# One more drain of GpSimd in the last unit of an attention and two-layer mixture-of-experts kernel

## The chip, the cores and the metric

The kernel runs on one core of one Trainium2 chip. The metric is the device time of a whole execution in microseconds. Three timed runs of the kernel before gave 915.9, 917.06 and 919.68, so its median is 917.06 us.

## The reference, cut to what matters

An attention with RMS-normed queries and keys gives 1792 rows of 768 values; two mixture-of-experts layers follow, and each sends every row through one of eight experts.

```python
x = attn_out.transpose(0, 2, 1, 3).reshape(B * S, H * D)      # 1792 x 768
# layer 1, and layer 2 with a bias per modality in its logits
e_idx = argmax(x @ w_gate, axis=1)
for e in range(8):
    mask = e_idx == e
    h = maximum(x[mask] @ w1[e], 0)          # 768 -> 1024
    out[mask] = gate[mask] * (h @ w2[e])     # 1024 -> 768
```

## The kernel before, in words

The attention takes the first 330 us. After it the rows of an expert are worked on in units of at most 304 or 128 rows. A unit (`M.unit`, with its body in `halves`) gathers its rows from DRAM with indirect DMAs of GpSimd (L340), multiplies them by `w1` in eight blocks (the first half), applies the relu, multiplies by `w2` in six blocks (the second half, tile `pl`), transposes each block back on TensorE (tile `pty`, L419), scales it on VectorE into `yr` (L420) and scatters `yr` to DRAM with one indirect DMA of GpSimd for each 128 rows (L370). The tile pool of `pty` has three buffers. The scatter of a unit is put off: it is issued in block 0 of the following unit, and that of the last unit by `M.flush()` after it.

The last six units of layer 2 are `seq`: four of up to 304 rows and two of up to 128. How many rows each expert got is known on the chip alone, so between the two halves of the last unit stands a branch (`others`, L1002) over code for experts with still more rows. With these inputs that code is not entered. Each engine jumps over it by itself, and on the way GpSimd raises the semaphores of its DMA queue by what the skipped code would have added (an instruction named INC_SWDGE_SEM in the trace). VectorE's first write of `yr` in the second half waits for semaphores that this instruction raises, since the earlier scatters must have read `yr`.

At the end of the program (L1038) SyncE waits for the last transfers, every engine runs a drain, an instruction without operands, and the engines meet in a barrier that GpSimd gathers. Then the semaphores are cleared and a second barrier follows. `side` is a table: for a unit and a step of it, functions that are called there. `pin` keeps the instructions of each engine in the order in which they were issued.

Of the kernel before, what the change touches and what calls it, by code (L numbers as in the profile page):

```python
# [805 lines left out]
def body_full(tc,q,k,v,g_q,g_k,wg,wog,w1,w2,mod,wg2,bias2,v1,v2,out,stop=False,O=None):  # L806
    nc=tc.nc
    with ExitStack() as ctx:
# [119 lines left out]
        def stepper(name):  # L928
            def f():
                if name not in S: S[name]=F[name]()  # L930
                next(S[name],None)
            return f
# [17 lines left out]
        sides={1:{KF+j:[stepper("table1")] for j in range(6)},2:{5:[stepper("pick2")]*2,**{j:[stepper("pick2")] for j in range(6,14)}},3:{2:[ns1],5:[stepper("pick3")]*2,**{j:[stepper("pick3")] for j in range(6,14)}}}  # L950
# [43 lines left out]
        def load(t,n): return nc.values_load(t[0:1,0:1],min_val=0,max_val=n)  # L994
# [10 lines left out]
                M.redo(seq[-1],None)  # L1005
            M.slot=sl; M.post=post
        def known(): S["over"]=load(over,E+G2)
        sides={0:{KF+i:[stepper("table3")] for i in range(6)},1:{2:[more]},4:{2:[known]}}
        for j,u in enumerate(seq):
            M.unit(u,nx=seq[j+1] if j<5 else None,fx=seq[j+2] if j<4 else None,side=sides.get(j),late=0,mid=others if j==5 else None)  # L1010
        M.flush()
# [30 lines left out]
```

## Time and profile before

| | us |
|---|---|
| median of three timed runs | 917.06 |
| the profiled execution, its own time | 913.84 |
| its span, first to last instruction | 912.1 |
| PE busy | 837.5 (92% of the span) |
| POOL (GpSimd) busy | 386.4 (42%) |

Times in the rows below count from the start of the span. An engine's name with a q (POOLq, SPq) stands for its sequencer: what it runs without the engine's datapath, such as waits for semaphores, branches, register moves and drains. A row of POOL ends when GpSimd has issued a transfer, not when the data has landed.

### The profile page before, as it was taken

The page shows a single profiled execution, that of the slowest core. Times are in us where ns is not written, and L with a number is a line of the kernel's source. Part 1 is how long each engine was busy: PE and PEld are TensorE (multiplying, and loading weights), DVE is VectorE, ACT ScalarE, POOL GpSimd, SP SyncE. Part 2 cuts the span into 40 slices and gives each one's busy share as a digit, 9 for nine tenths or more (in the row PEclk, how much of TensorE's full clock was granted, in tenths as well). Part 3 has the DMA queues.
Part 4 walks back from the last instruction along what each step waited for, and adds up shares of the span by engine and source line. Part 5 has one row for each costly group of instructions (what it writes and reads, how often), then busy time and mean ns, then how long its engine had stood idle before and what let it go on. Part 6 is the DMA issues. An engine that isn't in the chain of part 4 may idle for free. (4 is left out here: it accounts for less than half of the span.)

```text
span 912.1 us, 23363 instructions
## 1 busy us (share of the span) xinstructions
PE 837.5 (92%) x8881; PEld 657.4 (72%) x8898; DVE 681.6 (75%) x1416; ACT 526.2 (58%) x967; POOL 386.4 (42%) x404
## 2 busy tenths in 40 slices
PE   4699999998998899899999999989989999999974
PEld 1365766666655688777888898987767788777864
DVE  6688888888778784777797888888656686655780
ACT  4586776776766642565455666655435554544660
POOL 5686777777766522412243232343031522402110
PEclk9799999999999899899999999999999999999996
DMA  5577666666555554987659679778647797694750
GB/s 131 124 168 186 157 158 176 166 155 167 120 150 154 131 178 134 304 232 299 190 197 318 188 246 324 242 219 303 191 146 240 251 328 192 239 269 138 273 184 8
DMA packets 143939, 181.91 MB, mean 199 GB/s; under 512 B 73737, under 2 KB 111385, under 8 KB 143809
## 3 DMA queue, kind: packets, MB, share of 16 engines
q1 hardware_dynamic: 135712, 157.45, 58.4%
q0 software_dynamic: 6784, 22.32, 7.6%
q8 instruction: 73, 1.20, 0.6%
q10 hardware_dynamic: 1312, 0.47, 0.2%
q14 instruction: 58, 0.47, 0.2%
HBM read 130.12 MB, written 24.33 MB: 169 GB/s over the span
## 5 line engine op out<-in xcount | busy, mean ns | idle before, releaser
L361 PE MATMUL pl<-XT,w1h 128*128 128x304 f16 (+7 forms) x1632 | 252.3, 263 | 2.2 <-DVE hl L365 0.9
L361 PE MATMUL pl<-hh,w2h 128*128 128x304 f16 (+7 forms) x816 | 213.7, 273 | 7.3 <-DVEq L1002 3.6
L361 PE MATMUL pl<-hh,w2l 128*128 128x304 f16 (+7 forms) x816 | 213.2, 272 | 0.0
L361 PE MATMUL pl<-XT,w1l 128*128 128x304 f16 (+7 forms) x816 | 210.0, 269 | 1.3 <-DVE w1l L299 1.3
L361 PE MATMUL pl<-hl,w2h 128*128 128x0 bf16 x816 | 206.5, 258 | 2.6 <-DVE hl L365 2.6
L361 PEld LDWEIGHTS <-w2h 128*128 128x128 f16 x1632 | 151.9, 100 | 33.0 <-ACTq L972 3.9
L361 PEld LDWEIGHTS <-w1h 128*128 128x128 f16 x1632 | 149.8, 98 | 26.3 <-issue 3.4
L652 POOL TENSOR_TENSOR plo<-p 128x448 f16<-128x448 f32 x142 | 140.3, 1006 | 50.7 <-ACT p L649 47.3
L299 DVE TENSOR_TENSOR w1l<-r,w1h 128x1024 bf16<-128x1024 f32 x96 | 116.6, 1229 | 44.1 <-ACT w1h L298 43.9
L429 ACT COPY yt<-pl 128x304 f32<-128x304 f32 (+7 forms) x102 | 37.1, 364 | 152.3 <-PE pl L361 152.3
L345 POOL TENSOR_TENSOR XS<-xr,XS 128x768 bf16<-128x768 f32 (+5 forms) x27 | 47.9, 1794 | 167.8 <-ACT XS L344 156.6
L298 ACT CAST w1h<-r 128x1024 f16<-128x1024 f32 x96 | 99.6, 1054 | 0.1
L649 ACT ACTIVATE p<-pst,eb 128x896 f32<-128x896 f32 (+1 forms) x96 | 86.4, 911 | 14.2 <-PE pst L645 13.3
L361 PEld LDWEIGHTS <-w2l 128*128 128x128 bf16 x816 | 82.0, 100 | 16.5 <-issue 3.7
L364 ACT ACTIVATE hh<-pl 128x304 f16<-128x304 f32 (+7 forms) x136 | 50.4, 373 | 73.6 <-PE pl L361 70.1
L662 PE MATMUL av<-vv,p 128*128 128x65 f16 (+1 forms) x768 | 89.2, 198 | 2.0 <-ACT xrow L674 2.0
L361 PEld LDWEIGHTS <-w1l 128*128 128x128 bf16 x816 | 80.6, 99 | 14.3 <-DVE w1l L299 1.6
L662 PEld LDWEIGHTS <-p 128*128 128x128 bf16 (+1 forms) x768 | 73.2, 102 | 20.9 <-issue 14.8
L664 PE MATMUL av<-vv,plo 128*128 128x65 f16 (+1 forms) x768 | 87.4, 195 | 0.6 <-DVE plo L652 0.6
L663 PE MATMUL av<-vv,p 128*128 128x64 f16 (+1 forms) x768 | 87.9, 197 | 0.0
L626 DVE TENSOR_REDUCE m<-psm 128x2 f16<-128x896 f32 x70 | 76.0, 1086 | 8.3 <-PE psm L621 6.5
L299 DVE TENSOR_TENSOR w2l<-raw,w2h 128x768 bf16<-128x768 f32 x64 | 73.3, 1145 | 9.1 <-ACT w2h L298 8.4
(309 smaller groups left out, 1661.0 us busy)
## 6 DMA issues: line engine op xcount, KB each, us to landing
r<-in_moe_w_dram SPq DMA_DIRECT2D x96, 512.0 KB, 8.9
raw<-in_moe_w_dram SPq DMA_DIRECT2D x64, 384.0 KB, 5.5
r2a<-in_moe_w_dram SPq DMA_DIRECT2D x32, 384.0 KB, 7.5
r2b<-in_moe_w_dram SPq DMA_DIRECT2D x32, 384.0 KB, 6.6
T<-Z SPq DMA_DIRECT2D x48, 224.0 KB, 3.5
T<-Z SPq DMA_DIRECT2D x48, 112.0 KB, 3.1
yd<-zero SPq DMA_DIRECT2D x14, 384.0 KB, 3.1
rv<-in_v_dram SPq DMA_DIRECT2D x24, 192.0 KB, 3.5
```

The costliest lines, as they stand in the source:

```text
L298: if part!=1: nc.scalar.copy(h,t)
L299: if part!=0: (eng or nc.vector).tensor_tensor(out=l,in0=t,in1=h,op=ALU.subtract)
L345: if part!=0: (eng or nc.vector).tensor_tensor(out=self.XS[:m,t,1].bitcast(BF16),in0=x,in1=h,op=ALU.subtract)
L361: self.nc.tensor.matmul(o,a,b,start=i==0,stop=i==tot-1); i+=1
L364: nc.scalar.activation(h,p,AF.Relu)
L429: nc.scalar.copy(self.yt[:,db,:N],p)
L626: if t<3: nc.vector.tensor_reduce(m[:,t:t+4:3],p[:,:,:S],axis=AX.X,op=ALU.max,negate=True)
L649: self.nc.scalar.activation(self.d["P",i][:,self.u(kt)],p[:,:nn,:S],AF.Exp,bias=self.eb,scale=0.125)
L652: eng.tensor_tensor(out=self.d["L",i][:,u],in0=P[:,u],in1=self.hi(P)[:,u],op=ALU.subtract)
L662: nc.tensor.matmul(o,hh,w[:,0:65],start=kt==0,stop=False)
L663: nc.tensor.matmul(o[:,0:64],hh,w[:,65:129],start=False,stop=False)
L664: nc.tensor.matmul(o,ll,w[:,0:65],start=False,stop=kt==3)
```

## The change

One entry is added to the table `sides`: in the last unit (5), at step KF, which is the first block of its second half, `nc.gpsimd.drain` is called once.

```diff
-        sides={0:{KF+i:[stepper("table3")] for i in range(6)},1:{2:[more]},4:{2:[known]}}
+        sides={0:{KF+i:[stepper("table3")] for i in range(6)},1:{2:[more]},4:{2:[known]},5:{KF:[nc.gpsimd.drain]}}
```

The built program has one instruction more, a drain without waits or semaphores of its own, on GpSimd. All other instructions of the five engines, and their semaphores, are as before. The drain does not stand where the text of the kernel calls it. A drain reads and writes no tile, and in the built program it stands a little earlier: behind the scatter of the last unit but one and ahead of the branch over the extra units. The rows of GpSimd there, which list no drains and read the same before and now, are (`over` is the count that the branch tests, `s2ni` the first load of the code that is jumped over):

```order
L994 TENSOR_LOAD over
L370 DMA out_dram<-yr,idx_88 1792x768
L1002 COMPARE_AND_BRANCH
L994 TENSOR_LOAD s2ni
L997 COMPARE_AND_BRANCH
```

The added drain is between the second and the third of these. Where the branch lands, GpSimd has these rows, again the same in both: the instruction that raises the semaphores, the last scatter and the end of the program.

```order
L1002 UNCONDITIONAL_BRANCH
L1002 ISA
L1002 UNCONDITIONAL_BRANCH
L370 DMA out_dram<-yr,idx_85 1792x768
L1038 UNCONDITIONAL_BRANCH
```

Between the added drain and the first drain of the end GpSimd therefore issues one transfer, the last scatter.

## Rows read from the trace of the kernel before

**Rows 1.** Chain of waits from 880 us on; columns are start, length, what.

```profile
885.61 14.98 issue
900.59 1.21 POOLq L1038
```

**Rows 2.** Line L1038, the end; min/median/max in ns, first and last start.

```profile
L1038 SPq EVENT_SEMAPHORE  x13: 17/28/18507, 885.2 to 912.1; - x13
L1038 POOLq EVENT_SEMAPHORE  x4: 17/17/17, 911.3 to 912.0; - x4
L1038 POOLq DRAIN  x3: 46/109/10682, 900.6 to 911.8; - x3
L1038 SPq DRAIN  x3: 7/7/13, 904.3 to 911.5; - x3
```

**Rows 3.** Stages of the end: busy us of PE, PEld, DVE, ACT, POOL; clock, DMA share, GB/s.

```profile
902.00:904.00 2.00, 0.00 (x0) 0.00 (x0) 0.00 (x0) 0.00 (x0) 0.00 (x0) 0.57 0.21 80
904.00:911.30 7.30, 0.00 (x0) 0.00 (x0) 0.00 (x0) 0.00 (x0) 0.00 (x0) 0.50 0.00 0
911.30:912.10 0.80, 0.00 (x0) 0.00 (x0) 0.00 (x0) 0.00 (x0) 0.00 (x0) 0.50 0.00 0
```

**Rows 4.** Timeline of POOL, its last two instructions; start, length, what, idle before.

```profile
879.65 1.64 POOL L370 DMA_INDIRECT out_dram<-yr,idx  x1 [9.80 <-DVE hl L365]
900.82 0.98 POOL L370 DMA_INDIRECT out_dram<-yr,idx  x1 [19.53 <-DVE yr L420]
```

**Rows 5.** Line L1027, the start of the program; columns as in Rows 2.

```profile
L1027 POOLq INC_SWDGE_SEM  x1: 27/27/27, 0.2 to 0.2; - x1
...
L1027 POOLq DRAIN  x1: 182/182/182, 0.4 to 0.4; - x1
```

**Rows 6.** Timeline of POOL around an indirect DMA of the attention.

```profile
286.75 1.82 POOL L652 TENSOR_TENSOR plo<-p 128x448 f16<-128x448 f32 x2
288.73 1.26 POOL L155 DMA_INDIRECT o<-payc,rt_ixi  x1 [0.16 <-issue]
289.99 1.85 POOL L652 TENSOR_TENSOR plo<-p 128x448 f16<-128x448 f32 x2
```

**Rows 7.** POOL's groups of indirect DMAs; count, busy us, mean ns, idle before.

```profile
L370 POOL DMA_INDIRECT yd<-yr,idx x19 | 24.5, 1290 | 43.4 <-DMA yd<-yr,idx 21.1 <-DVE yl L432 8.1 <-DMA pay<-o 5.2
L370 POOL DMA_INDIRECT out_dram<-yr,idx x20 | 24.5, 1224 | 87.5 <-DVE yr L420 43.6 <-DMA out_dram<-yr,idx 30.8 <-DVE hl L365 12.4
L155 POOL DMA_INDIRECT o<-rt_pay,rt_ixi x19 | 22.1, 1163 | 37.1 <-DMA o<-rt_pay,rt_ixi 21.9 <-DVE hl L365 12.3 <-POOL rt_pay L144 2.9
L340 POOL DMA_INDIRECT xr<-yd,idx x20 | 21.7, 1085 | 39.2 <-DVE yr L420 19.6 <-DVE hl L365 14.8 <-issue 3.9
L340 POOL DMA_INDIRECT xr<-xd,idx x19 | 21.2, 1115 | 25.8 <-ACT lt L456 10.3 <-DVE idx L335 7.0 <-ACT hh L364 4.3
L155 POOL DMA_INDIRECT o<-payc,rt_ixi x16 | 17.6, 1097 | 28.0 <-DMA o<-payc,rt_ixi 14.7 <-DVE hl L365 8.4 <-DVE pk_mx L176 2.3
```

**Rows 8.** Line L1002, GpSimd's way over the branch; columns as in Rows 2.

```profile
L1002 POOLq EVENT_SEMAPHORE  x5: 17/43/62, 882.3 to 882.6; - x5
...
L1002 POOLq COMPARE_BRANCH  x1: 62/62/62, 879.4 to 879.4; - x1
L1002 POOLq INC_SWDGE_SEM  x1: 2450/2450/2450, 882.7 to 882.7; - x1
```

**Rows 9.** Timeline of DVE, first and last write of `yr` in the second half.

```profile
894.06 0.29 DVE L420 TENSOR_TENSOR yr<-pty,pay 128x128 f32<-128x128 f32 x1 [5.96 <-PE pty L419]
...
900.25 0.29 DVE L420 TENSOR_TENSOR yr<-pty,pay 128x128 f32<-128x128 f32 x1 [0.33 <-PE pty L419]
```

**Rows 10.** Timeline of PE, first and fourth transpose of the same half.

```profile
893.60 0.42 PE L419 MATMUL pty<-ident,yt 128*128 128x128 f32 x1
...
898.10 0.28 PE L419 MATMUL pty<-ident,yt 128*128 128x128 f32 x1
```

## The prediction

> **What bounds the kernel now.** Over the whole span TensorE does, but the change touches GpSimd in the last 33 us, so I read the end first. The chain of waits [rows 1] shows GpSimd waiting 14.98 us for the last block of `yr`, and then its drain of line L1038 as the last piece. The line itself [rows 2] gives that drain 10.682 us, from 900.59 to 911.27; the other two drains of GpSimd at the end took 0.109 and 0.046 us. I take the long one to be the first, since GpSimd's next semaphore instruction starts at 911.3. SyncE's long wait for the transfers ended at 885.2 + 18.5 = 903.7, and its first drains ran at 904.3; the second was over at about 904.4. So from 904.4 everybody waits for GpSimd. The stage table [rows 3] says what happens meanwhile: between 904.0 and 911.3 no engine is busy and the DMA engines move nothing. These 911.27 - 904.40 = 6.87 us are the time that the change can reach. After the drain 912.12 - 911.27 = 0.85 us of barriers remain.
>
> **What the long drain may be.** The last scatter ran from 900.82 to 901.80 [rows 4], and the data moved before 904 [rows 3]. The drain goes on for 911.27 - 901.80 = 9.47 us behind the scatter's row. It is not the bare instruction: a drain at the program's start, ahead of any transfer, took 0.182 us [rows 5], and the two short ones above follow a drain directly. It is not GpSimd still at work on one transfer either: in the attention an operation that needs the whole engine starts right behind an indirect DMA (288.73 + 1.26 = 289.99) and takes the usual 0.92 us [rows 6]. So it is something that a drain alone waits for or does, and that the previous drain leaves clean. Two readings fit. In the first the drain settles what all transfers since the last drain have left behind. There were 19 + 20 + 19 + 20 + 19 + 16 = 113 indirect ones [rows 7], which makes 9.47 / 113 = 0.084 us each. A cost that is paid once, at the first drain after any transfer, gives the same result. In the second reading each drain that follows a transfer, even a single one, costs some 9.5 us. No row of this trace shows a drain behind a single transfer, so the rows don't decide.
>
> The Trainium skill speaks for a third reading. PSUM — Partial Sum Buffer, section "Engine vs sequencer instructions", says that a drain waits for the engine to go fully idle, and nothing more. By that rule the added drain of an idle GpSimd does nothing for the one at the end, and the sum would be zero. The trace does not agree with the rule as it stands, since POOL's last row ended 9.47 us before the drain did [rows 2, 4].
>
> **The change part by part.** It adds one drain to GpSimd and moves nothing else. The parts are the cost where it stands, and what the drain at the end costs afterwards.
>
> Where it stands: the drain comes behind the scatter of 879.65 and ahead of the branch. In the kernel before GpSimd's sequencer reached the branch at 879.4, the scatter's row ended at 881.29 [rows 4], and the semaphore instruction ran from 882.7 to 885.2 [rows 8]. From the branch to its end are 885.2 - 879.4 = 5.8 us, most of it the way to the new code. The price of the added drain lies between 0.05 us (the shortest one in rows 2) and, behind a scatter with 112 transfers already made, the 9.47 us of the long one or more. I take 9.47, the only row of a drain behind transfers. Then it ends at 881.29 + 9.47 = 890.8, and the semaphores are raised at 890.8 + 5.8 = 896.6. Queued behind it on GpSimd is only the last scatter, which waits for `yr` until 900.59 [rows 1] and so loses nothing. VectorE is the one who waits for the semaphores: its first write of `yr` goes from 894.06 to about 896.6 and ends at 896.9 [rows 9]. Behind it stand the five other writes, of 0.29 us each, of which two are late by then and catch up. TensorE notices only when its fourth transpose at 898.10 finds none of the three `pty` buffers free [rows 10], and the first one is free at 896.9. The cost is 0 with 898.1 - 896.9 = 1.2 us to spare. Without that cover each further microsecond of the added drain would move the end by one.
>
> At the end: call f the time from the last scatter's row to the end of the last long drain, 9.47 now. Below 2.6 us (904.40 - 901.80) it no longer counts, because SyncE's wait for the landing comes last. So the gain is 9.47 - max(2.6, f). f lies between 0.05 and 9.47 by the rows, or above if another drain cost something, for which nothing speaks. Under the first reading it is 0.084 us for one transfer, or 1.9 us if the drain waits for the landing until 903.7. In both cases the gain is the full 6.87 us. I take the first reading: the cost is nowhere seen beside single transfers, though 113 of them are issued, and it is gone at the next drain.
>
> The sum is 0 + (-6.87): 913.84 - 6.87 = 906.97 us for the profiled execution, with a span near 905.2. The median of the runs shown lies 3.2 us above the profiled execution, and I forecast a median: 917.06 - 6.87 = 910.2 us.
>
> **The rivals.**
>
> No change: each drain behind a transfer costs about 9.5 us, or the drain at the end holds something of its own. For it: all rows fit, since every short drain in the trace follows either no transfer or another drain, and the added drain has a scatter behind it. Against it: 9.47 us is about ten times the 0.98 us in which the scatter was issued [rows 4], and the data had moved before 904 [rows 3]. The time is then 917.06, since the added drain itself is covered by the 1.2 us. By the PSUM page's rule above it would be the same; that is a part of this rival's chance.
>
> A part of the gain: a fixed part of 5 to 8 us in every drain behind a transfer, the rest from the backlog. f is 5 to 8, the gain 1.5 to 4.5 us, the time 912.6 to 915.6. Nothing in the rows speaks for a split, and nothing against it.
>
> Slower: the added drain holds GpSimd longer than 9.47 + 1.2 = 10.7 us behind the scatter of 879.65, for instance because the first one after 112 transfers pays more than the last one does. From that point VectorE's first write of `yr` comes too late for TensorE's fourth transpose, and TensorE stands. With twice the price, 18.94 us, the drain ends at 900.2, the first `yr` at 900.2 + 5.8 + 0.3 = 906.3, and the end moves by 906.3 - 898.1 = 8.2 us if the drain at the end is not shortened: 917.06 + 8.2 = 925.3. Shortened, the two nearly cancel. Against it: the drain of the kernel before settled as many transfers and needed 9.47.
>
> That the change does not do what it says is part of the first rival: the drain stands ahead of the branch and not in the second half, but still behind the last transfer but one, so a backlog would be settled all the same.
>
> **How the numbers follow.** The forecast has a chance of 0.50, no change 0.38, a part of the gain 0.07, slower 0.05. A change under 0.5%, here 4.6 us, can't be told from none in a measurement of this kernel. The forecast's 6.87 us lie outside that bound, and the partial gain inside it. What the scatter of the runs carries over that bound between the first two cases I leave even; 0.01 of no change may read as slower. That makes 0.50 for faster, 0.38 + 0.07 - 0.01 = 0.44 for the same and 0.05 + 0.01 = 0.06 for slower. The likeliest case has a range of its own from 908.7 to 912 us. The range for 8 in 10 takes in the forecast and most of no change: from 908.4 to 918.5; the tail of no change and the slower case are left out.
>
> **What would show it.** If right, the long drain moves to about 879.4 to 890.8, VectorE's first `yr` comes near 896.6, TensorE's transposes stay where they are, and the first drain of L1038 ends by 904, so that SyncE's drain is the last to arrive. If a drain costs 9.5 us behind any transfer, both drains will be long and the 7.3 us stretch without work stays. If the added drain is short and the last one long, the cost belongs to the end of the program or to the last transfer. The prediction is wrong if the last drain still ends more than 4.9 us behind the last scatter's row, or if TensorE waits for a `pty` buffer.

## The result and the profile after

| | before | after |
|---|---|---|
| median of six timed runs, us | 918.68 (915.9 to 919.68) | 907.74 (902.84 to 910.78) |
| ratio | | 0.9878 [0.9846, 0.991] |
| the profiled execution, us (span) | 913.84 (912.1) | 907.44 (905.7) |

The brackets behind a ratio are its 95% interval. The change made the kernel faster, as forecast. The median lies 0.66 us below the lower end of the range, and the six runs put the gain at 10.9 us where 6.9 were forecast. The trace comes first, then the question whether the rest is real.

The end of the chain of waits of the kernel after (start, length, what) has the same last piece as [rows 1]. The step to the last scatter now goes through the semaphores of L1002:

```profile
871.78 24.91 DMA out_dram<-yr,idx
896.70 0.10 POOLq L1002
897.21 3.88 issue
901.09 1.20 POOLq L1038
```

The added drain has a line of its own in the trace, L389 (columns as in [rows 2]):

```profile
L389 POOLq DRAIN  x1: 11253/11253/11253, 882.3 to 882.3; - x1
```

It ended at 893.51. The end of the program, answering to [rows 2]:

```profile
L1038 SPq EVENT_SEMAPHORE  x13: 17/28/7397, 896.8 to 905.6; - x13
L1038 POOLq EVENT_SEMAPHORE  x4: 17/17/17, 904.9 to 905.6; - x4
L1038 POOLq DRAIN  x3: 50/109/3190, 901.1 to 905.4; - x3
L1038 SPq DRAIN  x3: 7/7/13, 904.8 to 905.1; - x3
```

The long drain of 10.682 us is now one of 3.190 us, from 901.09 to 904.28. SyncE's wait for the transfers ended at 896.8 + 7.4 = 904.2, so drain and landing end together. GpSimd's last scatters, answering to [rows 4]:

```profile
882.49 1.63 POOL L370 DMA_INDIRECT out_dram<-yr,idx  x1 [9.81 <-DVE hl L365]
901.33 0.97 POOL L370 DMA_INDIRECT out_dram<-yr,idx  x1 [17.20 <-DVE yr L420]
```

The added drain ended 893.51 - 884.12 = 9.39 us behind the first of these, the drain at the end 904.28 - 902.30 = 1.98 us behind the second. The stage table (columns as in [rows 3]) has lost the stretch of 7.3 us without work. What is left of it is 1.5 us, the barriers included:

```profile
902.40:904.20 1.80, 0.00 (x0) 0.00 (x0) 0.00 (x0) 0.00 (x0) 0.00 (x0) 1.00 0.23 89
904.20:905.70 1.50, 0.00 (x0) 0.00 (x0) 0.00 (x0) 0.00 (x0) 0.00 (x0) 0.64 0.00 0
```

From the end of the last scatter's row to the end of the span were 912.12 - 901.80 = 10.32 us before, and are 905.71 - 902.30 = 3.41 us now: 6.91 us less. The scatter itself came 0.50 us later, and 6.91 - 0.50 is the difference of the two spans, 6.4 us.

GpSimd's way over the branch, answering to [rows 8]:

```profile
L1002 POOLq EVENT_SEMAPHORE  x5: 17/43/43, 896.2 to 896.5; - x5
...
L1002 POOLq COMPARE_BRANCH  x1: 62/62/62, 893.5 to 893.5; - x1
L1002 POOLq INC_SWDGE_SEM  x1: 172/172/172, 896.6 to 896.6; - x1
```

INC_SWDGE_SEM fell from 2.450 to 0.172 us, which no step of the prediction had. The writes of `yr` and the transposes, answering to [rows 9, 10]; VectorE first:

```profile
897.19 0.82 DVE L420 TENSOR_TENSOR yr<-pty,pay 128x128 f32<-128x128 f32 x3 [7.31 <-DMA out_dram<-yr,idx]
...
900.75 0.29 DVE L420 TENSOR_TENSOR yr<-pty,pay 128x128 f32<-128x128 f32 x1 [0.33 <-PE pty L419]
```

and TensorE, first, fourth and last transpose:

```profile
894.97 0.28 PE L419 MATMUL pty<-ident,yt 128*128 128x128 f32 x1
...
898.61 0.28 PE L419 MATMUL pty<-ident,yt 128*128 128x128 f32 x1
...
900.39 0.33 PE L419 MATMUL pty<-ident,yt 128*128 128x128 f32 x1 [0.29 <-ACT yt L429]
```

VectorE held three blocks back and wrote them at a stretch from 897.19. The first `pty` buffer was free at about 897.5, 1.1 us before TensorE's fourth transpose, which shows no wait. In this execution the added drain cost nothing.

Elsewhere the two executions differ by the clock. Before the end, from 850 to 890 and from there on, the kernel before:

```profile
850.00:890.00 40.00, 32.69 (x511) 29.53 (x511) 30.99 (x51) 25.79 (x50) 6.72 (x5) 0.94 0.57 198
890.00:912.00 22.00, 9.92 (x147) 9.44 (x145) 1.75 (x6) 1.59 (x6) 0.98 (x1) 0.66 0.02 8
```

and the kernel after:

```profile
850.00:890.00 40.00, 33.82 (x527) 29.76 (x527) 32.42 (x52) 27.03 (x52) 6.72 (x5) 1.00 0.64 225
890.00:905.70 15.70, 9.02 (x150) 8.62 (x150) 1.66 (x6) 1.60 (x6) 0.97 (x1) 0.86 0.05 14
```

The granted clock (third column from the right, a mean over stretches at 1.2 and at 2.4 GHz, which are 0.5 and 1.0 here) was 0.94 and 0.66 before, 1.00 and 0.86 after. The last scatter but one came 882.49 - 879.65 = 2.84 us later than before, the last one only 0.50 us. TensorE's instructions between them are the same in both kernels, and from the end of the one scatter's row to the fourth transpose the mean clock was 0.78 before and 0.88 after. So I put the 2.3 us to the clock, which no run of its own shows; they are no part of the gain of 6.91 us.

### The profile page after: what moved, and what is told of

The parts are those of the page before. It is cut to its first block, busy times and chain, and to the rows that moved or that the text cites. A ratio compares the mean times of both kernels' runs of the same rounds, so it can differ in the third digit from the quotient of the medians.

```text
span 905.7 us, 23364 instructions
## 1 busy us (share of the span) xinstructions
PE 835.3 (92%) x8881; PEld 653.9 (72%) x8898; DVE 680.9 (75%) x1416; ACT 527.2 (58%) x967; POOL 387.3 (43%) x404
## 5 line engine op out<-in xcount | busy, mean ns | idle before, releaser
L361 PE MATMUL pl<-XT,w1h 128*128 128x304 f16 (+7 forms) x1632 | 249.7, 261 | 3.2 <-issue 1.0
L361 PE MATMUL pl<-XT,w1l 128*128 128x304 f16 (+7 forms) x816 | 207.9, 267 | 1.3 <-DVE w1l L299 1.3
L361 PEld LDWEIGHTS <-w2l 128*128 128x128 bf16 x816 | 81.1, 99 | 17.2 <-issue 4.2
```

What stands on the lines that cost most here:

```text
L361: self.nc.tensor.matmul(o,a,b,start=i==0,stop=i==tot-1); i+=1
```

## The experiments

The theory: a drain of GpSimd takes a time for each transfer of GpSimd's queue made since the last drain, and at least until the last one has landed (the backlog theory). Rivals: a fixed price behind any transfer, a price paid once by the first drain behind a transfer, a cost of the program's end, and, for the first result's size, a further gain that the trace of one execution does not show. Counts below include two plain transfers at the start beside the 113 indirect ones of [rows 7], 115 in all.

### How much it gains: the changed kernel again, and the drain one scatter earlier

`again` is the changed kernel without an edit.

> The changed kernel once more, for the size of its gain. In the profiles the gain sits at the end: from the end of the last scatter's row to the end of the program 10.3 us before (912.12 - 901.80) and 3.4 us after (905.71 - 902.30), 6.9 us less. If that is all, the timed ratio comes near 0.9925 (0.990 to 0.995), and the 10.9 us between the medians so far were 4 us of scatter from stretches at the lower clock. If something else in the program gained as well, the ratio stays near 0.988 and the gain beyond 7 us must show in the spans of a stage before the last unit. Backlog theory: added drain 11.2 us, last long drain 3.2 us again.

Measured: 909.99 us median of 12 runs (904.43 to 913.78) against 915.91 of 23 (910.99 to 922.17), ratio 0.9942 [0.9919, 0.9965]. The trace has the same drains, 11.257 and 3.193 us.

`unit4` puts the drain one scatter earlier:

```diff
-4:{2:[known]},5:{KF:[nc.gpsimd.drain]}}
+4:{2:[known],KF+5:[nc.gpsimd.drain]}}
```

> The drain is placed one scatter earlier: behind the three scatters of the fourth unit of 304 rows, ahead of the scatter of the last unit but one. Two transfers are left to the drain of the end. Backlog theory: added drain still about 9.3 us behind the last scatter's row before it, last drain within 0.2 us of the landing, time equal to the changed kernel (ratio to before 0.9925), the semaphore instruction at the branch near 0.2 us, and VectorE's first write of yr no longer late. Theory of a fixed price for each drain behind a transfer: the same kind of gain would be missing, 9.5 us at the end.

Measured: 908.34 us median of 12 runs (903.7 to 914.86), ratio 0.9919 [0.989, 0.9947]. Its drains:

```profile
L389 POOLq DRAIN  x1: 10294/10294/10294, 874.0 to 874.0; - x1
L1038 POOLq DRAIN  x3: 46/109/3247, 905.0 to 909.4; - x3
```

The added one, behind 113 transfers, ended 10.18 us behind the row of the last of them. The one at the end, behind two transfers, ended at 908.29, 2.05 us behind the last scatter's row and not twice 1.98; SyncE's wait for the landing ended at 908.2 here. So behind one or two transfers the landing sets its end. VectorE's first `yr` was on time, 898.59. The intervals of the two kernels overlap: no further gain of an earlier drain is shown, as its former place was covered.

The forecast's 6.87 us are a ratio of 1 - 6.87/917.06 = 0.9925. It lies in both intervals of these larger sets and outside that of the first six pairs. Over all three sets of runs of the kernel before (46 runs) the median is 917.1 us and the standard deviation 2.7; over both of the kernel after (18 runs) 909.4 and 3.1. The medians of the sets of one kernel are up to 2.8 us apart (915.91, 917.78 and 918.68 before). So the 10.9 us were most likely 6.9 and the scatter of two medians of six; over all runs the medians are 7.7 us apart.

### Once, or for each transfer: an early drain, and one in the middle

`early` is the kernel before with a drain among the first instructions, behind the two plain transfers:

```diff
-            M.set_caps(CAPS,((128,0),(N2,128)))
+            M.set_caps(CAPS,((128,0),(N2,128))); nc.gpsimd.drain()
```

> One drain at the end of GpSimd's constants, behind two plain transfers and ahead of all 113 indirect ones. Theory of a price paid once, at the first drain after the library is loaded or after any transfer: the drain at the end becomes short (about 3.2 us), time some 7 us less. Backlog theory: the drain of the end still lasts 9.5 us behind the last scatter's row, time as before; the early drain itself takes under 2 us.

Measured: 919.83 us in one run. Its early drain and its last:

```profile
L826 POOLq DRAIN  x1: 684/684/684, 12.5 to 12.5; - x1
...
L1038 POOLq DRAIN  x3: 56/105/10505, 906.8 to 917.8; - x3
```

```profile
907.00 0.97 POOL L370 DMA_INDIRECT out_dram<-yr,idx  x1 [19.67 <-DVE yr L420]
```

The last drain began at 906.76 and ended 9.31 us behind the last scatter's row (907.96). The price is not paid once. 113 transfers instead of 115 cost 9.31 instead of 9.47 us, 0.08 each.

`l1u4` is the kernel before with a drain in the middle, in a unit of layer 1, behind 63 transfers and ahead of 52:

```diff
+4:{KF:[nc.gpsimd.drain]}      # entry in the table of layer 1's units
```

> One drain in the middle, in the fifth large unit of layer 1: 63 transfers of GpSimd before it, 52 behind it. Backlog theory at 0.084 us a transfer: the added drain lasts 63 x 0.084 = 5.3 us behind the row ahead of it, and the drain of the end 52 x 0.084 = 4.3 us behind the last scatter's row (9.47 before), so the end comes 5.1 us earlier. Theory of a price paid once: the added drain 9.4 us, the last one 2.0 us. Theory of a price by drain: both near 9.4.

Measured: 914.54 us in one run.

```profile
L389 POOLq DRAIN  x1: 12898/12898/12898, 551.4 to 551.4; - x1
L1038 POOLq DRAIN  x3: 52/109/5522, 906.4 to 912.5; - x3
```

The last scatter's row is 906.63 + 0.97, so the last drain ended 4.32 us behind it, as expected: 52 x 0.083. A price of the program's end, or a fixed price, would have left 9.5. A price by the time since the last drain doesn't fit either: 342 us of 900 are 0.38, and 4.32 of 9.47 is 0.46, as is 52 of 115 (0.45). The middle drain was a miss: it ended at 564.32, 9.65 us behind the row of the transfer before it, where 5.3 were expected. These are that row and the two halves of that time in the stage table:

```profile
553.68 0.99 POOL L340 DMA_INDIRECT xr<-xd,idx  x1 [0.31 <-issue]
```

```profile
554.70:559.90 5.20, 5.20 (x58) 5.00 (x56) 4.46 (x7) 3.03 (x7) 0.00 (x0) 1.00 0.97 320
559.90:564.30 4.40, 4.40 (x52) 4.24 (x50) 3.27 (x6) 3.31 (x8) 0.00 (x0) 1.00 1.02 345
```

All 16 DMA engines were busy for the whole of it (share 0.97 and 1.02), while during the drain of the changed kernel the share was 0.04. In `unit4` it was 0.93, and that drain took 10.18 us for 113 transfers where the price gives 9.31. So a drain under other transfers takes longer. The landing alone doesn't make the difference: by its semaphore's updates in the trace the last gather of `l1u4` had landed at 561.69, 7.02 us behind its row, and the drain ended 2.63 us after that. What fills those is open.

`both` has the drain of `l1u4` and that of the changed kernel.

> A drain in the middle (after 63 transfers) and the drain of the change (51 transfers later). The second one shows a middle count while the DMA engines have little to do: 51 x 0.0824 = 4.2 us behind the scatter ahead of it, if the 0.0824 us hold and the 9.65 us of the middle drain in the run before (63 transfers, DMA engines fully busy) came from the traffic. If a transfer costs 0.15 us in any middle drain, 7.7 us. The drain of the end near 2.0 us, and VectorE's first yr no longer late.

Measured: 911.01 us in one run.

```profile
L389 POOLq DRAIN  x2: 6112/9604/13097, 550.2 to 884.5; - x2
L1038 POOLq DRAIN  x3: 50/109/3193, 904.7 to 909.0; - x3
```

The row of the scatter that the second one stands behind:

```profile
884.73 1.64 POOL L370 DMA_INDIRECT out_dram<-yr,idx  x1 [9.73 <-DVE hl L365]
```

The middle drain is long again, and again it ended 2.63 us after its last gather had landed (560.71 and 563.34). The second, 6.112 us, ended 4.24 us behind its scatter's row (886.37) for 51 transfers (0.083 each, DMA share 0.02 meanwhile). The backlog's price holds inside the program too, where the DMA engines are idle. The drain of the end took 1.99 us behind the last row, and VectorE's first `yr`, at 898.39, was on time, both as expected.

### What settles the backlog: other transfers

`plain1` has, where the changed kernel has its drain, one small transfer of GpSimd from a tile of zeros to scratch. It does no useful work.

```diff
+        def plain(): nc.gpsimd.dma_start(out=M.dr.tile([16,8],F32,name="ex"),in_=M.zero[:16,:8])
-5:{KF:[nc.gpsimd.drain]}}
+5:{KF:[plain]}}
```

> No added drain. In its place, behind the scatter of the last unit but one, one small plain transfer of GpSimd (16 partitions, 8 values each, to a scratch tensor nobody reads). If a plain transfer settles what earlier ones left, the drain at the end has two or three left and ends with the landing, about 2.0 us behind the last scatter's row: the gain of the changed kernel (ratio to before 0.992 to 0.994) with GpSimd held for under 2 us instead of 9.4, and VectorE's first yr on time. If it does not settle them, the drain takes 116 x 0.0824 = 9.6 us and the time is as before.

Measured: 917.88 us median of 12 runs against 917.78 of 17, ratio 0.9999 [0.9974, 1.0024].

```profile
L1039 POOLq DRAIN  x3: 46/109/10821, 911.0 to 922.4; - x3
```

```profile
911.26 1.03 POOL L370 DMA_INDIRECT out_dram<-yr,idx  x1 [17.81 <-DVE yr L420]
```

It ended 9.55 us behind the last scatter's row, behind 116 transfers. A transfer in the drain's place settles nothing: it is the drain that does. The one transfer more cost 0.08 us, though it has 16 rows; by rows (16 of 128) it would have been about 0.01. The added drain of the changed kernel ended 9.39 us behind its scatter in three executions (`again` and `hold` below among them), so 0.08 us is no scatter.

`more128` and `more16` are the kernel before with 42 more such transfers, of 128 or 16 partitions, in units of layer 1; `ind42` has 42 indirect ones. The edit shown is that of `more128`.

```diff
+        ex=M.dr.tile([42*128,8],F32,name="ex")
+        def extra():
+            i=S.get("ex",0); S["ex"]=i+1
+            nc.gpsimd.dma_start(out=ex[i*128:(i+1)*128,:],in_=M.zero[:128,:8])
+        sides.update({g:{j:[extra] for j in range(14)} for g in (4,5,6)})
```

The expectations of `more128` (its "the same" is `more16`), `more16` and `ind42`, in this order:

> The same with 128 partitions in each of the 42 transfers. By transfers and by rows: 157 x 0.0824 = 12.9 us. By bytes: 42 x 4 KB against the 22 MB of the others, 9.5 us. The semaphore instruction at the branch of the last unit, 2.45 us before, goes with the same count: 0.17 + 156 x 0.020 = 3.3 us.

> The kernel before with 42 more plain transfers of GpSimd in layer 1, each from 16 partitions to DRAM (8 values a partition, to a scratch tensor nobody reads). If the drain at the end pays by transfers, it lasts 157 x 0.0824 = 12.9 us behind the last scatter's row (9.47 before). If it pays by rows, 42 transfers of 16 rows count as 5 of 128 and it lasts 9.9 us. If it pays by time or by something fixed, 9.5 us.

> The kernel before with 42 more transfers of GpSimd in layer 1, this time indirect ones (128 rows of 8 values to scratch tensors nobody reads). With 42 plain ones the drain at the end took 3.4 and 3.8 us behind the last scatter's row instead of 12.9, and the semaphore instructions of these runs (0.172 us + 0.020 us for each transfer left) say that some 36 and 45 were left of 157. If plain transfers settle what earlier ones left, and indirect ones don't, all 157 are left here: the drain 157 x 0.0824 = 12.9 us behind the last scatter's row, the semaphore instruction of the last unit 0.17 + 156 x 0.020 = 3.3 us. If instead a full list settles itself at some number near 115 to 130, the drain is far shorter, 2 to 4 us, here too.

Measured: 920.64, 920.8 and 964.66 us, one run each. (The 42 indirect transfers made the kernel longer ahead of the end: INC_SWDGE_SEM behind layer 1 starts at 735.7 us, 681.1 before.) The drains at the end were shorter than both expectations for the plain transfers said; that of `ind42` came out as its second case, a list that settles itself. That of `more128`, and its two INC_SWDGE_SEM:

```profile
L1043 POOLq DRAIN  x3: 46/165/5011, 912.6 to 918.6; - x3
```

```profile
L977 POOLq INC_SWDGE_SEM  x1: 541/541/541, 692.9 to 692.9; - x1
L1007 POOLq INC_SWDGE_SEM  x1: 1057/1057/1057, 895.0 to 895.0; - x1
```

It ended 3.81 us behind the last scatter, that of `more16` 3.43, that of `ind42` 3.80, where 157 transfers at 0.082 would be 12.9. INC_SWDGE_SEM tells when the list had become short. In the other kernels the one of the last unit took 0.172 us behind no transfer since a drain, 0.192 behind one, 1.190 behind 51 and 2.450 behind 114: 0.172 + 0.020 for each. The one behind layer 1 took 0.028 us more than that (0.680 behind 24, 1.940 behind 87). In `more128` the one behind layer 1, behind 129 transfers, took 0.541, which reads as 17, and the one of L1007, behind 156, took 1.057, or 44. So most of the list was settled once without a drain, in `more128` and `ind42` at about the 112th transfer and in `more16` some nine later, while it never was in kernels with 115 or 116. The number alone doesn't decide it, then; what does is open. As the list was cut short, these three also leave open how rows or bytes count for larger transfers.

`cover` and `coverind` are the changed kernel with the same 42 transfers, and were to use up the cover by a longer drain.

> The changed kernel with the same 42 transfers. The added drain lasts 156 x 0.0824 = 12.9 us instead of 9.4 behind the scatter ahead of it, which is 3.5 us more than in the changed kernel, and there the first write of yr was 898.61 - 897.48 = 1.1 us ahead of TensorE's fourth transpose. So the cover is used up: VectorE's first yr comes 3.5 us later, TensorE's fourth transpose waits for a buffer for about 2.3 us, and the last scatter comes 2.3 us later against the start of the second half. The drain at the end stays near 2.0 us behind the last scatter's row. If the cover were larger than I think, the transposes stay 1.2 us apart.

> The changed kernel with the same 42 indirect transfers, to use up the cover of the added drain. If all are left: added drain 156 x 0.0824 = 12.9 us behind the scatter ahead of it, 3.5 us more than in the changed kernel, where the first write of yr was 898.61 - 897.48 = 1.1 us ahead of TensorE's fourth transpose. TensorE's fourth transpose then waits about 2.3 us for a buffer, and the last scatter comes that much later against the start of the second half; the drain at the end stays near 2.0 us. If the list settles itself, the added drain is short and the transposes stay 1.2 us apart.

Measured: 911.77 and 964.01 us. The added drains took 5.542 and 5.548 us and ended 3.67 us behind their scatter, as the list had been settled here too (the second case of `coverind`; `cover` had only the other); the last ones took 3.196 and 3.191. The cover was not reached, so these two say nothing on it.

### The cover: GpSimd held longer

`hold` is the changed kernel with twelve memsets of a scratch tile and a second drain behind the added one. They serve only to keep GpSimd from the branch.

```diff
-5:{KF:[nc.gpsimd.drain]}}
+5:{KF:[nc.gpsimd.drain,lambda: [nc.gpsimd.memset(dm,0.0) for _ in range(12)],nc.gpsimd.drain]}}
```

> The added drain is followed by twelve memsets of GpSimd on a scratch tile of 128x256 f32 (0.310 us each in a row of the kernel before, 3.7 us together) and a second drain, so that GpSimd reaches the branch, and raises its semaphores, about 3.7 us later than in the changed kernel; nothing else is changed. If VectorE's first write of yr is covered by 1.1 us ahead of TensorE's fourth transpose, as I read it (897.48 against 898.61 in the changed kernel's trace), then that cover is used up: the first write comes about 3.7 us later, measured from the first transpose (5.9 instead of 2.2 us behind it), the fourth transpose comes 6.2 instead of 3.6 us behind the first, the last scatter about 2.6 us later, and the time is about 912.6 against 910.0. The second drain of the pair should be short (it follows a drain and no transfer), and the last drain about 3.2 us as before. If TensorE or VectorE has more slack than I read, the fourth transpose stays 3.6 us behind the first and the time near 910. The single time moves by some us with the granted clock, so the distances in the trace decide.

Measured: 914.71 us in one run at a mean clock of 0.966, beside 914.37 of the kernel before at 0.979; two single runs, so the distances in the trace decide. Its drains and memsets (the line's drains, then GpSimd's timeline):

```profile
L389 POOLq DRAIN  x2: 398/5826/11255, 886.0 to 901.4; - x2
```

```profile
886.28 1.63 POOL L370 DMA_INDIRECT out_dram<-yr,idx  x1 [9.77 <-DVE hl L365]
897.38 4.38 POOL L1008 MEMSET dm<- 128x256 f32 x12 [9.46 <-issue]
```

The first drain is that of the changed kernel (9.39 us behind the scatter), the second, behind it and no transfer, took 0.398 us, the end of the memsets included. The last one, at the program's end, took 3.197 us, as expected. VectorE's first writes of `yr`, and TensorE's first, third and fourth transpose:

```profile
905.41 1.07 DVE L420 TENSOR_TENSOR yr<-pty,pay 128x128 f32<-128x128 f32 x4 [10.79 <-PE pl L361]
```

```profile
900.62 0.42 PE L419 MATMUL pty<-ident,yt 128*128 128x128 f32 x1
...
903.87 0.28 PE L419 MATMUL pty<-ident,yt 128*128 128x128 f32 x1
905.85 0.30 PE L419 MATMUL pty<-ident,yt 128*128 128x128 f32 x1 [0.60 <-DVE yr L420]
```

The first write came 905.41 - 887.91 = 17.5 us behind the scatter's row, 4.4 us more than in the changed kernel (897.19 - 884.12 = 13.1). The fourth transpose now waits for `yr`, 0.60 us. Without the wait it would have come 1.21 us behind the third, at 905.08 (the distance in the changed kernel), so 0.8 us reached TensorE and 3.6 were covered. 1.1 covered and 2.6 paid were expected. The place is the one I named; its size goes with TensorE's pace. From the scatter's row to the fourth transpose were 16.8 us in the kernel before, 14.5 in the changed one and would have been 17.2 here, at a mean clock of 0.78, 0.88 and 0.78: shorter where less of it lay at the lower clock. GpSimd's way from the drain's end to the raised semaphores kept its time, 3.3 us in the changed kernel and 3.2 here.

## Why the prediction was right, and where it was wrong

**What the drain does: right.** The added drain took what the one at the end had taken, and the one at the end only the landing of its transfer. The backlog reading holds with 0.082 to 0.083 us for each transfer when the DMA engines are otherwise idle: 9.47 us for 115, 9.31 for 113, 4.32 for 52, 4.24 for 51, and 1.98 for one, by the landing. The 0.084 of the prediction came from 113, without the two plain transfers. Of the two values that f was given for one transfer, 0.084 and 1.9 us, it was the second. `early` rules out that the price is paid once.

**The gain at the end: right.** 6.87 us forecast, 6.91 in the traces, 0.9942 and 0.9919 as ratios where 0.9925 was forecast.

**The cost in its place: zero was right, the way to it was not.** The drain ended 9.39 us behind its scatter's row, for 9.47 forecast. From the branch to the raised semaphores I carried over 5.8 us; they were 3.3 (893.5 to 896.8), since INC_SWDGE_SEM shrinks with the backlog too. On the other side the time from the scatter to TensorE's fourth transpose was 2.3 us shorter in this execution. The two errors cancel, and the cover of 1.1 us reads like the 1.2 forecast. With the old 2.45 us TensorE would have waited for about 1 us here, an estimate from 897.48 + 2.28 against 898.61. So the zero was in part luck, and `hold` shows that such a cover changes from execution to execution: 3.6 us there. It also shows that the wait lands where the rival "Slower" put it.

**The rivals.** No change: refuted, the second drain was not long. The rule of the Trainium skill, page PSUM — Partial Sum Buffer, section "Engine vs sequencer instructions", that a drain waits for the engine to go idle, gave the same; the trace does not agree, since GpSimd's engine had been idle for 9.39 us when the added drain ended. A part of the gain, with a fixed 5 to 8 us: refuted by 1.98. Slower: the added drain stayed under the 10.7 us from which it would have decided.

**Where it was wrong: the range, in the step "How the numbers follow".** I gave the likeliest case 908.7 to 912 us and the whole range a lower end of 908.4, 1.8 us under the forecast. The start of the sum was not the fault: the median of 46 runs is 917.1, where the three had 917.06, and all 18 runs of the changed kernel put it at 909.4, near the 910.2 of the forecast. What failed is the allowance for the scatter of the runs. All it had to go by were three runs, 3.8 us apart. The single runs have a standard deviation of 2.7 us before and 3.1 after, and a median of six runs of the changed kernel was at 907.74, one of twelve at 909.99, with the same drains in the traces. So the term of 6.87 us stands, and the allowance was mis-sized: by an estimate from these deviations it had to reach some 3 us to either side of 910.2, a lower end near 907.

**Not foreseen.** The price under busy DMA engines (9.65 us for 63 transfers) and the list that grows short by itself at some 112 to 121 transfers. Neither touches the change, since its drain runs while the DMA engines are idle and behind 114 transfers that had not been settled.

## What to carry to other kernels

Where a kernel issues many transfers on GpSimd's queue, look at the drain at the end: if it runs on long after the last landing, a second drain, put where GpSimd waits anyway, takes that time off the end. Count how much time there is up to the first engine that notices, and count it at either level of the clock. Where that is close, put the drain earlier: one scatter earlier gained no less here, and VectorE was not delayed. And take the width of a forecast from the scatter of many single runs, not from the distance of three.

## What the runs showed of the hardware

- With the DMA engines otherwise idle, a drain of GpSimd takes 0.082 to 0.083 us for each transfer of its queue since the drain before, counted from the row of the last transfer, with 1.98 us, the landing, as the least behind an indirect transfer; 0.398 us behind a drain and twelve memsets. Plain and indirect transfers count alike in two runs: one plain more cost 0.08 us (9.55 for 116), two plain less saved 0.16 (9.31 for 113).
- INC_SWDGE_SEM of the last unit took 0.172 us and 0.020 more for each such transfer.
- Under a DMA share near 1 a drain behind 63 transfers took 9.65 us where 5.2 would be expected, 2.63 of them after the last transfer had landed.
- With 157 transfers the list had been settled once without a drain, and the last one cost 3.4 to 3.8 us instead of 12.9.
- In one set of 23 runs the kernel before lies between 910.99 and 922.17 us, 11.2 us apart. In this set the time falls with the mean granted clock, 922.17 us at 0.958 and 910.99 at 0.977.
